# The opening of a Fourier-mixing and hard-swish kernel: x loaded ahead of the weights, dummy products between its pieces, and a first chunk of plain block products

## The chip, the cores and the metric

The kernel runs on one core of one Trainium2 chip, as one launch. The metric is the device time of that launch in microseconds (us). PE is TensorE, ACT is ScalarE, DVE is VectorE, POOL is GpSimd; SP and POOL issue the DMAs. PSUM is the memory, divided into banks, that TensorE's products land in. The granted clock is the share of full speed that TensorE's clock had; at half clock a pass of an fp32 product over 512 columns takes 0.86 us in these traces, at full clock 0.43. "Before" and "changed" are the two kernels compared.

## The reference, cut to what matters

```python
# x: (8, 3008, 256); w_in: (256, 2048); w_out: (2048, 256), all float32
X = np.fft.fft(np.fft.fft(x, axis=1), axis=2).real      # (8, 3008, 256)
h = X.reshape(24064, 256) @ w_in
g = h * np.clip(h + 3.0, 0.0, 6.0) / 6.0
out = g @ w_out
```

The kernel does the length-3008 transform as 47 x 64: a first transform over 47 points, a trip through DRAM, a second over 64 points; the transform over the 256 columns is folded into `w_in`. Two batch rows form a pair, so there are four pairs; each pair has chunks of 256 columns, and each chunk eight steps. The weights arrive with 64 bits an element, as float64 would need; their exponents and mantissas are taken apart and put together as fp32 on ScalarE, TensorE and VectorE, in 16 pieces of 512 KB. Three words recur: the fold of an x piece is VectorE's elementwise work on it ahead of the first transform, the fold of `w_in` is a group of eight TensorE passes, and a join is VectorE's multiplying of a weight piece's mantissa and exponent.

## The kernel before: the parts that matter

Dummy products keep TensorE's clock up where it has no work:

```python
def keep_awake(n):
    ps = ps_h.tile([P, 2 * TB], F32, tag="uv", name="awake")
    for i in range(n):
        nc.tensor.matmul(ps[:], ones[:], Z[:], start=True, stop=True)   # 128x512, fp32
```

The opening takes the eight pieces of x in order. Each brings one piece of weights and moves one through its stages:

```python
for c in range(NXC):                       # NXC = 8
    if c + 2 < NXC:
        load_x(first, c + 2)
    load_w(c + 2)
    if c < NXC - 1:
        fold_first(first, c)               # VectorE
    else:
        for part in range(2):
            fold(first, c, part, nc.vector)    # the odd piece: a longer fold
    on_scalar(c)                           # exponents of a weight piece
    on_vector(c)                           # its mantissa; joins the piece before
    for i in range(XC // 2):
        (stage1_first if c < NXC - 1 else stage1)(first, c, i)    # first transform
    on_tensor(c)                           # exponent product; folds w_in, mixes w_out
    # ... (cut: loads of a table and of a row of w_in)
load_g(first, 0)                           # results read back from DRAM
for j in range(NXC, 15):                   # seven more weight pieces
    # ... (cut: load_w)
    on_scalar(j)
    on_vector(j)
    keep_awake(1)
    on_tensor(j)
# ... (cut)
keep_awake(2)
for i in range(2):
    stage2(first, 0, i)                    # second transform
```

A step is `mlp1` (products u and v, then the activation), `combine` (sums on GpSimd) and `mlp2` (seven products of 256 columns, in the manner of Strassen, in place of eight, on blocks of `w_out` that were mixed beforehand):

```python
for s, (p, ck, fc) in enumerate(steps):
    # ... (cut: what runs beside, for the next pair)
    if s + AHEAD < len(steps):             # AHEAD = 2
        mlp1(*chunk(s + AHEAD))
    if s + 1 < len(steps):
        combine(*chunk(s + 1))
    # ... (cut: store of the last chunk)
    mlp2(*chunk(s))
```

## Time and profile before

| | before |
|---|---|
| time, median of 3 runs | 1981.34 us (1980.88 to 1983.05) |
| span in the profile | 1978.3 us |
| TensorE busy | 1949.1 us, 99% |
| second chunk's first output products start at | 134.96 us |
| TensorE idle from 135 to 1940 us | 4.7 us |

### The profile page before, as it was taken

Reading aid. Unit: us, or ns where it says so; the run is one execution under the profiler, and the core shown is the slowest. Engines: PE = TensorE matmul, PEld = TensorE weight load, DVE = VectorE, ACT = ScalarE, POOL = GpSimd, SP = SyncE. Lnnn points to the kernel's source line nnn. Section 1 sums busy time; section 2 is a strip of 40 time slices with the busy share of each in tenths; the row PEclk is TensorE's granted clock in tenths of the full one; section 3 lists DMA queues with packets and bytes.
Section 4 is the critical chain, followed back from the end, with each engine's and each line's share of the span. In section 5 each row is a group of like instructions: output and inputs, shape, how many; then the busy total and the mean of one; then the engine's idle time right before and its main releaser. Section 6 shows DMA issues by size and latency. Waiting matters only on the chain.

```text
span 1978.3 us, 27746 instructions
## 1 busy us (share of the span) xinstructions
PE 1949.1 (99%) x9178; PEld 1685.4 (85%) x9178; DVE 1433.5 (72%) x2775; ACT 687.9 (35%) x1164; POOL 1414.2 (71%) x1604
## 2 busy tenths in 40 slices
PE   8899999999999999999999999999999999999998
PEld 5588888888998888888898888888889888888887
DVE  5677767776787776776777776777678777777776
ACT  6533333333333333333333333333333333333332
POOL 4277778786687787777768877778667667666765
PEclk9999999999999999999999999999999999999999
DMA  9502211111111111221111221212110101111000
GB/s 307 136 26 61 51 41 46 49 49 35 27 36 51 41 49 48 54 59 24 36 32 30 63 55 44 56 41 54 37 22 23 30 14 25 26 24 28 17 20 20
DMA packets 149701, 93.31 MB, mean 47 GB/s; under 512 B 121739, under 2 KB 135055, under 8 KB 149558
## 3 DMA queue, kind: packets, MB, share of 16 engines
q1 hardware_dynamic: 139294, 57.86, 12.2%
q0 software_dynamic: 9472, 33.49, 5.9%
q8 instruction: 72, 1.18, 0.2%
q14 instruction: 71, 0.58, 0.1%
q10 hardware_dynamic: 792, 0.20, 0.0%
HBM read 54.19 MB, written 37.33 MB: 46 GB/s over the span
## 4 chain that ended last, share of the span: by engine, by line
PE 93%; DVE 2%; ACT 1%; issue 0%; DMA 0%; SPq 0%; DVEq 0%; ACTq 0%
PE acc L403 56%; PE v L334 16%; PE u L334 16%; PE ps L284 2%; PE ps L227 2%; DVE a L379 1%; DVE s L339 1%; ACT t L376 0%; ACT PM L509 0%; DVE o L461 0%; PE wps L574 0%; DVE u L360 0%; PE ps L224 0%; PE ex L514 0%; PE awake L597 0%
## 5 line engine op out<-in xcount | busy, mean ns | idle before, releaser
L393 POOL TENSOR_TENSOR c<-a 128x512 f32<-128x512 f32 (+1 forms) x383 | 478.2, 1248 | 431.4 <-PE acc L403 369.3
L403 PE MATMUL acc<-c,G 128*128 128x256 f32 (+1 forms) x3072 | 712.0, 375 | 0.0
L376 ACT ACTIVATE t<-u,half 128x512 f32<-128x512 f32 (+1 forms) x384 | 261.0, 680 | 1100.5 <-DVE u L349 1018.7
L403 PEld LDWEIGHTS acc<-c,G 128*128 128x128 f32 x3072 | 577.5, 190 | 72.7
L339 DVE SCALAR_TENSOR_TENSOR s<-qn,WN,u 128x256 f32<-128x256 f32 (+1 forms) x768 | 330.0, 471 | 354.3 <-PE u L334 354.0
L403 PE MATMUL acc<-a,G 128*128 128x256 f32 (+1 forms) x2304 | 551.2, 375 | 0.0
L403 PEld LDWEIGHTS acc<-a,G 128*128 128x128 f32 x2304 | 433.8, 190 | 55.9
L334 PE MATMUL v<-q,W 127*128 127x256 f32 (+1 forms) x1536 | 390.1, 376 | 4.4 <-DVE a L379 4.4
L334 PE MATMUL u<-q,W 128*128 128x256 f32 (+1 forms) x1536 | 388.3, 375 | 2.4 <-DVE a L379 2.1
L379 DVE SCALAR_TENSOR_TENSOR a<-t,u 128x512 f32<-128x512 f32 (+2 forms) x448 | 263.7, 600 | 104.9 <-ACT t L376 102.1
L334 PEld LDWEIGHTS u<-q,W 128*128 128x128 f32 x1536 | 285.7, 190 | 58.2 <-issue 14.8
L334 PEld LDWEIGHTS v<-q,W 127*128 127x128 f32 x1536 | 288.7, 190 | 45.1 <-DVE a L379 4.1
L393 POOL TENSOR_TENSOR c<-c,a 128x256 f32<-128x256 f32 (+1 forms) x383 | 274.8, 717 | 30.0
L393 POOL TENSOR_TENSOR c<-a,c 128x256 f32<-128x256 f32 (+1 forms) x383 | 274.6, 717 | 30.1
L349 DVE TENSOR_TENSOR u<-s,v 128x512 f32<-128x512 f32 x352 | 245.0, 696 | 37.7 <-PE v L334 0.8
L379 DVE SCALAR_TENSOR_TENSOR a<-t,v 128x512 f32<-128x512 f32 (+1 forms) x480 | 263.2, 564 | 0.0
L376 ACT ACTIVATE t<-v,half 128x512 f32<-128x512 f32 (+1 forms) x384 | 260.5, 678 | 0.0
L351 DVE TENSOR_TENSOR v<-v,s 128x512 f32<-128x512 f32 x352 | 243.7, 692 | 0.0
L393 POOL TENSOR_TENSOR r<-w,e 128x256 f32<-128x256 f32 (+1 forms) x94 | 90.8, 987 | 3.7
L411 ACT ACTIVATE e<-acc 128x512 f32<-128x512 f32 (+2 forms) x190 | 86.3, 545 | 3.4 <-PE acc L403 3.3
L461 DVE STREAM_TRANSPOSE o<-r 128x256 f32<-128x256 f32 (+1 forms) x192 | 72.5, 414 | 0.2
L239 ACT COPY z<-ps 96x512 f32<-96x512 f32 x64 | 37.2, 582 | 83.7 <-PE ps L227 65.2
(91 smaller groups left out, 780.2 us busy)
## 6 DMA issues: line engine op xcount, KB each, us to landing
out_dram<-o SPq DMA_DIRECT2D x746, 32.0 KB
zd<-z SPq DMA_DIRECT2D x32, 384.0 KB
g<-zd SPq DMA_DIRECT2D x48, 256.0 KB
xt<-in_x_dram POOLq DMA_DIRECT2D x21, 384.0 KB, 4.1
qn<-qd SPq DMA_DIRECT2D x19, 256.0 KB
st<-in_moe_w_in_dram POOLq DMA_DIRECT2D x8, 512.0 KB, 9.1
st<-in_moe_w_out_dram POOLq DMA_DIRECT2D x8, 512.0 KB, 5.1
xt<-in_x_dram POOLq DMA_DIRECT2D x7, 376.0 KB, 3.9
```

Of the source, the lines that this page charges most:

```text
L227: nc.tensor.matmul(ps[0:PZ], F[0:PR, 0:PZ], y[:, 2 * i:2 * i + 2, :], start=True, stop=True)
L284: nc.tensor.matmul(ps[:, blk, u * P:n].rearrange("p (b k) -> p b k", b=2), g[:, kk, blk * (P + 1):blk * (P + 1) + P], T[:, :, gr, blk, kk, ...
L334: nc.tensor.matmul(ps[:, i, 0:nq], W1[r, blk, f * P:(f + 1) * P], q[r, blk, of:of + nq], start=True, stop=True)
L339: nc.vector.scalar_tensor_tensor(s[:, i, 0:nq], qn[:, of:of + nq], WN[:, f:f + 1], u[:, i, 0:nq], op0=AL.mult, op1=AL.add)
L349: nc.vector.tensor_tensor(u[:], s[:], v[:], op=AL.add)
L351: nc.vector.tensor_tensor(v[:], v[:], s[:], op=AL.subtract)
L376: nc.scalar.activation(t, h, AF.Relu, bias=half[:], scale=scale)
L379: nc.vector.scalar_tensor_tensor(dst, t, 1.0, h, op0=AL.min, op1=AL.mult)
L393: (eng or nc.gpsimd).tensor_tensor(out, in0, in1, op=AL.add)
L403: nc.tensor.matmul(ch.acc[i // 2][:, i % 2, 0:ch.n], G[:, i, fc, :], mv, start=(fc == 0 and i % 2 == 0), stop=(fc == NF - 1), skip_group_c ...
L411: nc.scalar.mul(ch.e[:, k:i + 1, 0:ch.n], ch.acc[i // 2][:, 0:i + 1 - k, 0:ch.n], 1.0 / WS)
L461: nc.vector.transpose(o[:, 0:n // DH, h], ch.r[:, m, h, 0:n].rearrange("p (j i) -> p j i", i=DH))
```

## The change

What the code does, with its aims as I read them: x is asked for ahead of the weights, so that the first transform ends early; dummy products between the pieces keep the clock up while TensorE waits; the weights are made ready partly before the second transform and partly around the first chunk's steps; and the first chunk multiplies by the four plain blocks of `w_out`, eight products in place of seven, so that it needs no mixed blocks and no sums. The core of the diff, with cuts marked:

```diff
-    keep_awake(6)
+    keep_awake(13)
 # ... (cut)
+    order = [NXC - 1] + list(range(NXC - 1))
+    for c in order[0:6]:
+        load_x(first, c)
+    load_forward(first, order[6])
+    for k, c in enumerate(order):
         # ... (cut: folds, as before)
         for i in range(XC // 2):
-            (stage1_first if c < NXC - 1 else stage1)(first, c, i)
-        on_tensor(c)
+            (stage1_first if k > 0 else stage1)(first, c, i)
+        keep_awake(2)
+        # ... (cut: the other x loads, weight pieces 0 to 6 behind them)
+    head(0)                              # exponents and mantissa of a piece
+    for j in range(5):
+        exponent_b(j)
+        keep_awake(2)
+        exponent_c(j)
+        fold_all()
+        if j < 4:
+            head(j + 1)
+        join(j)
+        copy_all()
         # ... (cut)
+    DUE = [(7, 8), (9, 10), (11, 12), (13, 14), (15,), (), (), ()]
 # ... (cut: pieces 5 and 6 around mlp1 of step 0, with keep_awake(3))
+        if s < NF:                       # the first chunk, NF = 8
+            for j in DUE[s][:1]:
+                head(j)
+            copy_all()
+            mlp1(*chunk(s + 1))
+            for j in DUE[s][:1]:
+                tail(j)                  # exponent product, join, next load
+            for j in DUE[s][1:]:
+                head(j)
+            mlp2_first(*chunk(s))        # four products of 512 columns
+            for j in DUE[s][1:]:
+                tail(j)
+            fold_all()
+            if s >= 4:
+                mix_w_out(s - 4)         # now on GpSimd
```

The second pair's loads start eight steps later and come at one piece of x in 8 steps in place of 9.

More of the change, by code (lines that the diff above doesn't have):

```diff
@@ L51 @@
 NK1 = (N1 + 1) // 2
+B11, B21, B12, B22 = 0, 1, 3, 6
 PROD = ("P1", "P2", "-P4", "P5", "P7", "-P6", "P3")
@@ L124, in __init__, with x_tile @@
             self.g, self.q, self.qn = {}, {}, {}
-    def x_tile(pr, i):
+    def x_tile(pr, c, i):
+        i += 2 * (c if pr.p > 0 else (c + 1) % NXC)
         pool, tag = xpool, "x"
@@ L140, in load_forward @@
     def load_forward(pr, c):
-        xt = x_tile(pr, 2 * c)
+        xt = x_tile(pr, c, 0)
         nr = PR + 2 if pr.p < NP - 1 else PR
@@ L151, in load_partners @@
     def load_partners(pr, c):
-        xr = x_tile(pr, 2 * c + 1)
+        xr = x_tile(pr, c, 1)
         pr.xr[c] = xr
@@ L231, in evict_z @@
         if i == 0:
-            pool, tag = (gpool, "g") if pr.p == 0 and c % 3 == 2 else (zpool, "z")
+            pool, tag = (gpool, "g") if pr.p == 0 and c % 3 == 1 else (zpool, "z")
             pr.z[c] = pool.tile([PZ, XC, D], F32, tag=tag, name="z")
-            if c == 0:
+            if pr.zd is None:
                 pr.zd = dpool.tile([2, NK1, 2, NS, D], F32, tag="zd", name="zd")
@@ L311, in __init__ @@
             self.last = ck == NCK - 1
+            self.first = ck == 0 and pr.p == 0
             self.final = self.last and pr.p == NP - 1
@@ L393, in add, with mlp2_first @@
         (eng or nc.gpsimd).tensor_tensor(out, in0, in1, op=AL.add)
+    def mlp2_first(ch, fc):
+        a = ch.a.pop(fc)
+        for h in range(2):
+            if fc == 0:
+                ch.acc[h] = ps_a.tile([P, 2, TB], F32, tag="acc", name="acc")
+            for f in range(2):
+                nc.tensor.matmul(ch.acc[h][:], G[:, (B11, B12, B21, B22)[2 * f + h], fc, :], a[:, :, f],
+                                 start=(fc == 0 and f == 0), stop=(fc == NF - 1 and f == 1))
+        if fc == NF - 1:
+            ch.r = epool.tile([P, 2, 2, TB], F32, tag="r", name="r")
+            for h in range(2):
+                for m in range(2):
+                    nc.scalar.mul(ch.r[:, m, h], ch.acc[h][:, m], (1 - 2 * m) / WS)
     def mlp2(ch, fc):
@@ L486, in load_w @@
         kind, n, i = PIECES[j]
-        st = wpool.tile([P, 2 * WB], I32, tag="st", bufs=4, name="st")
+        pool, tag, bufs = (wpool, "st", 4) if j % 7 < 4 else (cpool, "c", None)
+        st = pool.tile([P, 2 * WB], I32, tag=tag, bufs=bufs, name="st")
         o = st[:].bitcast(moe_w_in.dtype)
@@ L511, in exponent_b @@
     def exponent_b(j):
-        ex = ps_h.tile([P, WB], F32, tag="uv", name="ex")
+        ex = ps_h.tile([P, WB], F32, tag="uv", name="ex") if starting[0] else bank([P, WB], "ex")
         for i in range(2):
@@ L537, in join @@
             return
-        b12 = wpool.tile([P, 2, P], F32, tag="b12", bufs=2, name="b12")[:] if i == 0 else None
-        for h, g in enumerate((block(n, 0), b12) if i == 0 else (block(n, 1), block(n, 6))):
+        for h, g in enumerate((B21, B22) if i else (B11, B12)):
             f, e = (t.rearrange("p (c q h e) -> h p c q e", c=2, h=2, e=DH)[h] for t in (frac, ex))
-            nc.vector.tensor_tensor(g.rearrange("p c (q e) -> p c q e", e=DH), f, e, op=AL.mult)
-        if i == 0:
-            w[PIECES[j]] = b12
+            nc.vector.tensor_tensor(block(n, g).rearrange("p c (q e) -> p c q e", e=DH), f, e, op=AL.mult)
     def block(j, i):
         return G[:, i, 2 * j:2 * j + 2, :]
-    def use_pair(j):
-        kind, n, _ = PIECES[2 * j]
-        if kind == "in":
-            fold_w_in(n)
-        else:
-            mix_w_out(n)
     def mix_w_out(j):
-        b12 = w.pop(("out", j, 0))
         g = [block(j, i) for i in range(7)]
-        tt = nc.vector.tensor_tensor
-        tt(g[3], g[0], b12, op=AL.subtract)
-        tt(g[5], g[6], g[3], op=AL.add)
-        tt(g[2], g[5], g[1], op=AL.subtract)
-        tt(g[4], g[6], b12, op=AL.subtract)
+        tt = nc.gpsimd.tensor_tensor
+        tt(g[4], g[B22], g[B12], op=AL.subtract)
+        tt(g[3], g[B11], g[B12], op=AL.subtract)
+        tt(g[5], g[B22], g[3], op=AL.add)
+        tt(g[2], g[5], g[B21], op=AL.subtract)
     def fold_w_in(n):
@@ L571, in fold_w_in @@
         for blk in range(2):
-            ps = bank([P, WB], "wps")
+            ps = bank([P, WB], "wps") if starting[0] else spare[blk]
             for i in range(2):
@@ L579, in copy @@
                 nc.scalar.copy(W1[:, blk, cs], sums[blk][:])
-            nc.sync.dma_start(out=wn[n:n + 1], in_=W1[P - 1:P, 1, cs])
+            nb = WB // P
+            for k in range(nb):
+                f = n * nb + k
+                nc.sync.dma_start(out=WN[:, f:f + 1], in_=W1[P - 1:P, 1, f * P:(f + 1) * P])
         copies.append(copy)
-    def load_wn(n):
-        nb = WB // P
-        nc.sync.dma_start(out=WN[:, n * nb:(n + 1) * nb], in_=wn[n].rearrange("(j p) -> p j", p=P))
     def load_t(gr):
@@ L591, in load_t, with keep_awake @@
             nc.sync.dma_start(out=T[b * N2:(b + 1) * N2, b, gr], in_=c_stage2[:, gr])
-    def keep_awake(n):
-        ps = ps_h.tile([P, 2 * TB], F32, tag="uv", name="awake")
+    def keep_awake(n, ps=None):
+        ps = ps_h.tile([P, 2 * TB], F32, tag="uv", name="awake") if ps is None else ps
         for i in range(n):
@@ L621, with head, tail, fold_all @@
         nc.scalar.copy(t, Z[r].unsqueeze(1).to_broadcast([N2, NG, 2 * TB]))
-    wn = dpool.tile([NWI, WB], F32, tag="wn", bufs=1, name="wn")
-    load_forward(first, 0)
-    load_partners(first, 0)
-    load_w(0)
-    load_x(first, 1)
-    load_w(1)
-    pending, copies = [], []
-    def on_scalar(j):
-        for i in pending:
-            exponent_c(i)
-        if j is not None:
-            exponent_a(j)
+    folds, copies = [], []
+    def head(j):
+        exponent_a(j)
+        mantissa(j)
+    def tail(j):
+        exponent_b(j)
+        exponent_c(j)
+        join(j)
+        if j + 7 < len(PIECES):
+            load_w(j + 7)
+        if j % 2 and PIECES[j][0] == "in":
+            folds.append(PIECES[j][1])
+    def fold_all():
+        while folds:
+            fold_w_in(folds.pop(0))
+    def copy_all():
         while copies:
             copies.pop(0)()
-    def on_vector(j):
-        if j is not None:
-            mantissa(j)
-        for i in pending:
-            join(i)
-    def on_tensor(j):
-        if j is not None:
-            exponent_b(j)
-        done = pending.pop() if pending else 0
-        if done % 2:
-            use_pair(done // 2)
-        if j is not None:
-            pending.append(j)
-    for c in range(NXC):
-        if c + 2 < NXC:
-            load_x(first, c + 2)
-        load_w(c + 2)
-        if c < NXC - 1:
+    order = [NXC - 1] + list(range(NXC - 1))
[3 more added lines that the diff above has]
+    for k, c in enumerate(order):
+        if k > 0:
             fold_first(first, c)
@@ L666 @@
                 fold(first, c, part, nc.vector)
-        on_scalar(c)
-        on_vector(c)
         for i in range(XC // 2):
-            (stage1_first if c < NXC - 1 else stage1)(first, c, i)
-        on_tensor(c)
-        if c == 0:
-            load_t(0)
-        if c in (4, 6):
-            load_wn(PIECES[c - 4][1])
-    load_g(first, 0)
-    for j in range(NXC, 15):
-        if j < 14:
-            load_w(j + 2)
-        on_scalar(j)
-        on_vector(j)
-        keep_awake(1)
-        on_tensor(j)
-    load_wn(PIECES[6][1])
-    load_wn(PIECES[8][1])
-    load_g(first, 1)
-    load_t(1)
-    keep_awake(2)
+            (stage1_first if k > 0 else stage1)(first, c, i)
+        keep_awake(2)
+        if k == 0:
+            load_partners(first, order[6])
+        elif k == 1:
+            load_x(first, order[7])
+            load_t(0)
+            for j in range(4):
+                load_w(j)
+        elif k in (4, 5):
+            for j in ((4, 5), (6,))[k - 4]:
+                load_w(j)
+    load_g(first, 0)
+    head(0)
+    for j in range(5):
+        exponent_b(j)
+        keep_awake(2)
+        exponent_c(j)
+        fold_all()
+        if j < 4:
+            head(j + 1)
+        join(j)
+        copy_all()
+        load_w(j + 7)
+        if j % 2 and PIECES[j][0] == "in":
+            folds.append(PIECES[j][1])
     for i in range(2):
@@ L692 @@
     starting[0] = False
+    spare = [ps_a.tile([P, WB], F32, tag="acc", name="spare") for blk in range(2)]
     chunks = [[Chunk(pr, ck) for ck in range(NCK)] for pr in pairs]
     NST = 2 * NF
-    after = {}
     def beside(p):
@@ L706, in beside @@
         cur = pairs[p]
+        late = 4 if p == 0 else 0
         if p == 0:
-            for f in (on_scalar, on_vector, on_tensor):
-                after.setdefault(1, []).append((f, (None,)))
-            for gr in range(2, NG):
-                after.setdefault(gr, []).append((load_t, (gr,)))
+            put(2, load_g, cur, 1)
+            for gr in range(1, NG):
+                put(gr + 1, load_t, gr)
             put(NF - 1, close_w)
@@ L721, in beside @@
                 put(NST * (gr - 2) + 12, load_g, cur, gr)
-            s2(NST * (gr - 1), cur, gr)
+            s2(NST * (gr - 1) + (late if gr == 1 else 0), cur, gr)
         if p + 1 < NP:
@@ L725, in beside @@
             for c in range(NXC):
-                put(9 * c, load_x, nx, c)
-                put(9 * c + 3, fold, nx, c, 0, nc.gpsimd)
-                put(9 * c + 5, fold, nx, c, 1, nc.gpsimd)
+                t = 2 * late + (9 - late // 4) * c
+                put(t, load_x, nx, c)
+                put(t + 3, fold, nx, c, 0, nc.gpsimd)
+                put(t + 5, fold, nx, c, 1, nc.gpsimd)
                 for i in range(XC // 2):
-                    put(9 * c + 8 + 3 * i, stage1, nx, c, i)
+                    put(t + 8 + 3 * i, stage1, nx, c, i)
             put(NST * (NG - 1) - 2, load_g, nx, 0)
@@ L747, in chunk @@
         return chunks[p][ck], fc
-    on_scalar(15)
-    on_vector(15)
+    DUE = [(7, 8), (9, 10), (11, 12), (13, 14), (15,), (), (), ()]
+    head(5)
     mlp1(*chunk(0))
-    mlp1(*chunk(1))
-    on_tensor(15)
-    combine(*chunk(0))
+    tail(5)
+    head(6)
+    keep_awake(3, spare[0])
+    tail(6)
     prev = None
@@ L760 @@
             f(*a)
-        if s + AHEAD < len(steps):
-            mlp1(*chunk(s + AHEAD))
-        if s + 1 < len(steps):
-            combine(*chunk(s + 1))
-        if prev and fc < 3:
-            finish(prev) if fc == 0 else store(prev, fc - 1)
-        mlp2(*chunk(s))
-        for f, a in after.get(s, ()):
-            f(*a)
+        if s < NF:
[13 more added lines that the diff above has]
+                mix_w_out(s - 4)
+            if s == NF - 1:
+                mlp1(*chunk(NF + 1))
+                combine(*chunk(NF))
+        else:
+            if s + AHEAD < len(steps):
+                mlp1(*chunk(s + AHEAD))
+            if s + 1 < len(steps):
+                combine(*chunk(s + 1))
+            if prev and fc < 3:
+                if fc > 0:
+                    store(prev, fc - 1)
+                elif not prev.first:
+                    finish(prev)
+            mlp2(*chunk(s))
         if fc == NF - 1:
```

## The prediction

> **What bounds the kernel now.** I read the page first, then busy time by stretch, then the chain of work in order of time up to 140 us, then the timeline of the opening on all engines.
>
> ```profile
> PE 1949.1 (99%) x9178; PEld 1685.4 (85%) x9178; DVE 1433.5 (72%) x2775; ACT 687.9 (35%) x1164; POOL 1414.2 (71%) x1604
> ...
> 0.00:10.00 10.00, 8.39 (x12) 3.29 (x12) 2.63 (x9) 7.47 (x5) 6.38 (x13) 1.00 0.81 220
> 10.00:54.00 44.00, 39.73 (x156) 25.41 (x157) 27.51 (x60) 27.28 (x50) 14.15 (x21) 0.94 1.00 314
> 54.00:77.00 23.00, 19.72 (x50) 8.12 (x49) 14.65 (x32) 16.03 (x27) 2.85 (x4) 0.97 0.74 187
> 77.00:92.00 15.00, 10.74 (x53) 8.24 (x52) 9.41 (x18) 6.26 (x10) 5.55 (x7) 0.92 0.33 82
> 92.00:135.00 43.00, 41.54 (x196) 35.92 (x195) 32.22 (x54) 14.13 (x24) 28.10 (x31) 0.99 0.05 15
> 135.00:1940.00 1805.00, 1800.31 (x8549) 1576.79 (x8548) 1320.74 (x2514) 606.60 (x1030) 1339.37 (x1508) 1.00 0.16 39
> ```
>
> The first line is the page's: TensorE is busy 99%. The others are stretches: their length, then busy time of PE, PEld, DVE, ACT and POOL, the granted clock, the DMA share and GB/s. From 135 us on TensorE idles 5 us in 1805, so nothing is to be won there, and the change touches only what lies before. So the question is one date: when does the second chunk's first output product start, and what TensorE work is left then? In the chain of work it is this:
>
> ```profile
> 92.06 3.53 PE acc L403 x14
> 97.31 3.02 PE acc L403 x14
> ...
> 129.34 3.02 PE acc L403 x14
> 132.37 0.86 PE ps L227 x2
> 133.23 0.86 PE u L334 x4
> 134.09 0.86 PE v L334 x4
> 134.96 3.02 PE acc L403 x14
> ```
>
> The first chunk's eight steps start their output products (seven Strassen-like products each) at 92.06 to 129.34, the second chunk's first at 134.96. That step carries the first products (u, v) of two steps ahead and one product of the next pair.
>
> The opening up to there, from the timeline (start, duration, what; in brackets the idle time before):
>
> ```profile
> 1.61 8.39 PE L597 MATMUL awake<-Z,ones 128*128 128x512 f32 x12 [1.61 <-DVE ones L601]
> ...
> 9.11 0.69 DVE L189 TENSOR_TENSOR y<-xt 94x508 f32<-94x508 f32 x1 [5.47 <-DMA xt<-in_x_dram,IX]
> ...
> 13.52 0.68 DVE L189 TENSOR_TENSOR y<-xt 94x508 f32<-94x508 f32 x1 [1.80 <-DMA xt<-in_x_dram,IX]
> ...
> 49.17 1.99 PE L227 MATMUL ps<-y,F 94*96 94x512 f32 x2 [2.87 <-DVE y L174]
> ...
> 71.64 1.40 ACT L509 ACTIVATE PM<-st,bias 128x512 uint8<-128x512 int16 x2
> 73.09 0.38 PE L514 MATMUL ex<-PM,E 128*128 128x512 f16 x1 [0.27 <-ACT PM L509]
> 73.50 0.58 ACT L518 ACTIVATE ex<-ex 128x512 int32<-128x512 f32 x1 [0.46 <-PE ex L514]
> 74.00 1.40 ACT L509 ACTIVATE PM<-st,bias 128x512 uint8<-128x512 int16 x2
> ```
>
> Six dummy products run to 10.0; x's first piece lands at 9.1, the second at 13.5 with a weight piece between. The first transform ends at 53.7 after an idle gap and half-speed products. A weight piece then cycles through ScalarE (1.40), TensorE, ScalarE in 74.00 - 71.64 = 2.36 us.
>
> **What the Trainium skill says.** "TensorE: Matmul & The Clock Gate", Part 1: the array's clock falls to half after an idle window of about 3.4 us and returns after a busy one. The trace agrees in kind: the gap of 2.87 us is followed by 1.99 us for what later takes 0.86 (132.37), and the first dummy passes come 0.86 apart, the later ones 0.43. Same page, Back-to-back issue gap: N/2.4 + 2.5 ns, 216 ns at 512 columns. The fp16 products of the trace keep it (0.21); an fp32 product is two records of 0.43 at 512 columns, so 0.86 us warm. I use the trace's. "SBUF — State Buffer", Who interferes with whom: a VectorE instruction with two SBUF inputs contends with GpSimd's reads. Here the four weight mixing operations take 0.42 each at 70 us, GpSimd idle, and 0.83 to 1.48 at 101 us, GpSimd busy. "DMA: Bandwidth & Descriptors", Issuing engines are not separate DMA queues: all share 16 engines; here they are saturated at 314 GB/s from 10 to 54 us.
>
> **The change part by part**, as one clock through TensorE's new order (which I read from the two built programs, the order of instructions with their waits):
>
> *Start.* 13 dummy products instead of 6: 14 more passes of 0.43 = +6.0, so they end at 16.0. The first x piece (now the last one, folded by the longer form, nine VectorE operations that took 2.95 us before) should land at 9 as now and be folded by 12: the dummies, not the data, set 16.0.
>
> *First transform.* The odd piece takes 2.15 warm (0.86 + 0.43 + 0.86), each of seven others eight passes of 0.43 = 3.43. After every piece two dummies of 0.86 = 1.71. x alone is 0.79 MB a piece, 2.5 us at 314 GB/s, and even with 0.39 MB of results written a piece, 3.8 us: x arrives faster than TensorE goes through a piece, 5.14 us. So the dummies sit on the path. 16.0 + 2.15 + 1.71 + 7 x 5.14 = 55.9; the last real product ends at 54.2 (before: 53.7). What the early x won is spent.
>
> *Five weight pieces before the second transform* (before: fifteen). ScalarE is free at 55.3 after the last eviction. Pieces 0 and 1: exponents 55.3 to 56.7, product to 57.2, next exponents to 59.1, product to 59.5, dummies to 61.0. Piece 2: product to 61.85, dummies to 63.4, fold of w_in (8 passes) to 66.8. Piece 3's product goes behind it, to 67.25; piece 4's exponents wait on ScalarE for the fold's copies (67.6), come at 68.1 to 69.5; product 69.95, dummies 71.45, second fold to 74.9. The results read back for the second transform (sent at 57.4 before, the same now) are long there. Second transform: 16 + 8 passes of 0.107 = 2.6 us, from 74.9 (before 77.4) to 77.5.
>
> *First chunk.* u, v of step 0 to 79.2, activations through 82.1; pieces 5 and 6 interleaved with three dummies (2.6); step 0's output products start at about 86, 6 us before today's 92.06. But each step now has four block products of 512 columns, 8 x 0.43 = 3.43, instead of 3.02 (+0.4 a step, +3.3 in all), one or two exponent products (0.43 each) and in two steps a fold (3.43), which all were done before today's step 0. TensorE's sum a step: 9.4, 9.4, 6.0, 6.0, 5.6, 5.2, 5.2, 5.2. Waits: one PSUM bank serves all exponent products, so piece 8's product waits for piece 7's join (idle about 1.6), piece 9 and 14 the like; I find about 5 us of idle in steps 0 to 4. Starts of output products: 86, 97, 107, 113, 121, 126, 131, 137. Then u, v of steps 8 (in step 7), 9 and 10, and the second chunk's first output product starts at 144.1, against 134.96: **+9.1**. Left over then: one half of the second transform and one first-transform product, 0.86 each, which now come 4 and 8 steps later: **+1.7**. Sum **+10.8**.
>
> *Off the path:* mixing on GpSimd (16 operations of about 0.72) takes VectorE's 1.7 to 4.2 us a block away, but TensorE waits for neither. The first chunk needs no combine.
>
> **Cross-check by TensorE work.** Before 144.1: real work 26.2 first transform, 6.9 exponents, 13.7 folds, 3.4 second transform, 19.0 for u and v, 27.4 outputs = 96.6; dummies 13 + 16 + 10 + 3 = 42 products: 14.4 with the slow start, then 29 x 0.857 = 24.9; in all 137.5 with the 1.6 of start-up. So even with no wait at all 137.5 - 135.0 + 1.7 = +4.2 us. Dummies grow from 17.9 (30 records now) to 39.3: +21.4. That exceeds what can be removed: idle 1.6 + 4.3 + 3.3 + 4.3 + 1.5 = 15.0 in the stretches above, and the slow clock's few us.
>
> **Rivals.** (1) The change wins: dummies only fill waits for x, and with an unbroken clock and an earlier step 0 the chunk comes earlier. For it: step 0 is earlier, and the half clock (0.92 to 0.97 in three stretches) goes. It would need x to take over 5 us a piece, but now pieces come each 4.5 us with 0.52 MB of weights between. If it held, -5 us: 1976. (2) The step waits are worse: the one bank and ScalarE's queue (per early step 2 x 1.96 of exponent work + 1.35 + 1.1 of copies = 6.4 us) bind, gaps of 3 us cool the clock again: +20, 2001. For it: each such gap cooled it before. Against: folds and dummies fill most. (3) GpSimd, mixing late (the last block waits for the last plain product), delays the second chunk's combine: +1 to 2.
>
> **Range and chances.** 1981.3 + 10.8 = 1992.1, so 1992. Floor +4.2 gives 1985.5; waits twice as long as I find give +16 and rival 2 up to 2001. Range 1986 to 2000. Two per cent is 40 us, half of all the opening up to step 0, so within 2% at 0.97; faster 0.01, slower 0.02.
>
> **What would show it.** Right: the second dummy group of the start ends at 16.0 with x folded by 12; first-transform pieces 5.1 us apart with no TensorE idle; second transform near 75; step 0's output near 86; second chunk's first near 144; span after it unchanged but for 1.7. Wrong: TensorE idle waiting for x in the first 50 us (dummies free), granted clock below 0.95 after 80 us, or a later stretch that lost or gained over 2 us.

## The result, and the profile after

| | before | changed |
|---|---|---|
| time, median of 4 runs | 1982.19 us (1980.88 to 1984.15) | 1998.17 us (1996.26 to 1998.33) |
| ratio | | 1.0078, 95% interval 1.0060 to 1.0095 |
| span in the profile | 1978.3 us | 1996.3 us |
| second chunk's first output products | 134.96 us | 149.40 us |

Ratios here are the mean time of one kernel's fast runs over that of the other's fast runs of the same rounds, so not quite the ratio of the medians quoted. The changed kernel is 16 us slower by the medians; inside 2%, and clear of noise.

Busy time by stretch of the changed kernel: start and end, length, then busy time of PE, PEld (weight loads), DVE, ACT and POOL with their counts, granted clock, DMA share, GB/s.

```profile
0.00:10.00 10.00, 8.39 (x14) 3.62 (x15) 2.19 (x8) 7.42 (x5) 6.57 (x13) 1.00 0.80 196
10.00:54.00 44.00, 44.00 (x167) 27.65 (x166) 14.22 (x34) 10.82 (x22) 10.90 (x16) 1.00 0.89 264
54.00:77.00 23.00, 22.48 (x75) 10.96 (x74) 7.89 (x14) 13.82 (x23) 3.04 (x5) 1.00 0.56 156
77.00:92.00 15.00, 13.30 (x44) 6.93 (x43) 12.19 (x23) 10.93 (x18) 2.29 (x4) 1.00 0.37 105
92.00:135.00 43.00, 39.72 (x119) 21.18 (x118) 33.06 (x61) 21.64 (x35) 11.18 (x14) 0.96 0.21 56
```

From 10 to 54 us TensorE is busy without a gap at full clock, where it idled 4.3 us before, and yet the first transform ends no earlier. DMA went the other way, from a share of 1.00 to 0.89: with TensorE full, the transfers have slack. The chain of work of the changed kernel, in order of time (start, length, what):

```profile
1.60 14.11 PE awake L609 x26
15.72 0.86 PE ps L231 x2
...
50.56 3.46 PE ps L204 x16
...
74.59 1.78 PE ps L288 x16
...
96.75 3.43 PE acc L408 x8
...
109.28 4.54 PE acc L408 x6
...
149.40 3.02 PE acc L424 x14
```

"awake" are dummies, "ps L204" is the first transform, "ps L288" the second, "acc L408" a step's plain products, "acc L424" the second chunk's first. The two dates of the last two rows are what the prediction did not have. Between them and the first lines, how TensorE and VectorE go through one piece of x:

```profile
22.88 1.88 PE L609 MATMUL awake<-Z,ones 128*128 128x512 f32 x4
23.08 0.68 DVE L193 TENSOR_TENSOR y<-xt 94x508 f32<-94x508 f32 x1 [3.79 <-PE ps L204]
23.69 0.68 DVE L194 TENSOR_TENSOR xt<-xt 94x508 f32<-94x508 f32 x1
24.29 0.17 DVE L195 TENSOR_TENSOR xt<-xt 94x8 f32<-94x8 f32 x1
24.60 0.60 PE L204 MATMUL ps<-xt,F 94*96 94x258 f32 x2
```

In brackets is the idle time before an instruction and what ended it. Before the change, the fold waited for "DMA xt"; now VectorE idles 3.79 us at each piece and what ends it is TensorE's own products. x is there; TensorE's queue is what x waits for, and the dummies are in that queue.

The span grew by 18.0 us. Of this, 14.4 us are in the date of the second chunk. The next 1.7 us are one second-transform half and one first-transform product (0.86 each) that now come after that date. Some 1.5 us more is a wait: over the next 370 us, TensorE waits for ScalarE to empty the one PSUM bank that both transforms share. First the kernel before, then the changed one (who waits for whom: us in total, times, longest):

```profile
PE ps L227 <- ACT q L287: 1.2, 2, 0.7
```

```profile
PE ps L231 <- ACT q L291: 2.7, 4, 0.7
```

These three make 17.6 of 18.0.

### The profile page after: what moved, and what is told of

The parts are those of the page before. It is cut to its first block, busy times and chain, and to the rows that moved or that the text cites. A ratio compares the mean times of both kernels' runs of the same rounds, so it can differ in the third digit from the quotient of the medians.

```text
span 1996.3 us, 27723 instructions
## 1 busy us (share of the span) xinstructions
PE 1971.9 (99%) x9184; PEld 1684.6 (84%) x9184; DVE 1427.8 (72%) x2759; ACT 687.8 (34%) x1164; POOL 1398.3 (70%) x1591
## 4 chain that ended last, share of the span: by engine, by line
PE 95%; DVE 2%; ACT 1%; issue 0%; DMA 0%; SPq 0%; DVEq 0%; ACTq 0%
PE acc L424 54%; PE v L339 16%; PE u L339 16%; PE ps L288 2%; PE ps L231 2%; PE awake L609 1%; PE ps L204 1%; PE acc L408 1%; DVE a L384 1%; DVE s L344 1%; ACT PM L532 0%; ACT t L381 0%; DMA out_dram<-o 0%; DVE o L482 0%; PE wps L587 0%
## 5 line engine op out<-in xcount | busy, mean ns | idle before, releaser
L398 POOL TENSOR_TENSOR c<-a 128x512 f32<-128x512 f32 (+1 forms) x375 | 467.5, 1247 | 401.0 <-PE acc L424 366.6
L424 PE MATMUL acc<-c,G 128*128 128x256 f32 (+1 forms) x3008 | 697.0, 375 | 0.0
L424 PEld LDWEIGHTS acc<-c,G 128*128 128x128 f32 x3008 | 565.4, 190 | 71.1
L424 PE MATMUL acc<-a,G 128*128 128x256 f32 (+1 forms) x2256 | 539.0, 375 | 0.0
L424 PEld LDWEIGHTS acc<-a,G 128*128 128x128 f32 x2256 | 424.1, 190 | 54.4
L398 POOL TENSOR_TENSOR c<-c,a 128x256 f32<-128x256 f32 (+1 forms) x375 | 268.4, 716 | 29.4
L398 POOL TENSOR_TENSOR c<-a,c 128x256 f32<-128x256 f32 (+1 forms) x375 | 268.2, 715 | 29.4
```

The lines of the kernel that those rows point to most:

```text
L398: (eng or nc.gpsimd).tensor_tensor(out, in0, in1, op=AL.add)
L424: nc.tensor.matmul(ch.acc[i // 2][:, i % 2, 0:ch.n], G[:, i, fc, :], mv, start=(fc == 0 and i % 2 == 0), stop=(fc == NF - 1), skip_group_c ...
```

## The experiments

Times are medians of four to six runs; the record holds no e9 or e10. The kernel before was run beside them each time: its median was 1980.3 to 1980.6 us in these rounds, so 1 to 2 us below that in the table above, and a ratio is safer than a difference of medians across rounds. By the ratio alone e2, e4 and e7 (1.0072 to 1.0075, each about 0.0014 either way) can't be told from the changed kernel (1.0060 to 1.0095); what is said of them rests on one trace each. The last column is the date at which the second chunk's output products start in the profiled run. Such a date has a scatter of its own: the 13 dummies of the start, the same in the changed kernel, e1, e4 and e7, took 14.11, 13.55, 13.18 and 13.54 us, so up to 0.9 us of a difference can be theirs.

| run | what it is | time, us | ratio to before | second chunk at |
|---|---|---|---|---|
| (changed) | | 1998.17 | 1.0078 | 149.40 |
| e1 | changed, no dummies between x pieces | 1988.79 | 1.0041 | 140.06 |
| e2 | changed, 9 dummies at the start | 1995.51 | 1.0074 | 146.35 |
| e4 | changed, no dummies in the weight loop | 1995.37 | 1.0072 | 146.69 |
| e6 | changed, all three | 1983.99 | 1.0023 | 135.26 |
| e3 | before, with dummies between x pieces | 1988.85 | 1.0039 | 143.81 |
| e5 | before, with the plain first chunk | 1979.88 | 1.0001 | 138.55 |
| e8 | before, odd x piece first | 1980.76 | 0.9997 | 138.01 |
| e7 | changed, other order of weight pieces | 1995.59 | 1.0075 | 147.23 |
| e13 | e6, that order, old pace of the next pair | 1986.45 | 1.0024 | 139.44 |
| e11 | before, fewer dummies | 1978.84 | 0.9988 | 136.74 |
| e12 | e11 with plain chunk and dummies in waits | 1978.62 | 0.9983 | 133.98 |
| e14 | e12 with x one piece further ahead | 1977.82 | 0.9980 | 132.85 |

The theory at the start was that of the prediction: the dummies lie on TensorE's path. The rivals were that they only fill waits, and that other parts of the change make the loss.

### e1: no dummies between the pieces of x

```diff
             (stage1_first if k > 0 else stage1)(first, c, i)
-        keep_awake(2)
```

> The changed kernel without the two dummy products after each of the eight x pieces. Theory (dummies are on TensorE's path, x arrives faster than it is used): 8 x 1.71 = 13.7 us go, less some waits for x since a piece of x with its results (1.18 MB) needs 3.8 us of DMA against 3.43 of TensorE: 10 to 13.7 us less than the changed kernel, 1984 to 1988, the second transform starting at 61 to 65. Rival (dummies filled waits for x or kept the clock up): 0 to 3 us less, 1995 to 1998, with TensorE idle before each piece or a granted clock well below 1 from 16 to 55 us.

It took 9.4 us off, by the medians, and 9.3 off the date. So the dummies are on the path, and the rival (0 to 3 us) falls; but I had expected 10 to 13.7. What bounds it now, in its chain of work:

```profile
21.41 10.04 DMA zd<-z
...
32.62 12.11 DMA zd<-z
```

These are the writes of the first transform's results to DRAM. With the dummies gone TensorE is ahead, the DMA share in that stretch is 0.99, each write takes over 10 us to land, and its buffer, one of few, is wanted again. I had counted the bytes a piece, but put them at a wait for x; the wait that came was for the results' buffers. The granted clock fell to 0.92 there, and that cost 1.1 us on the chain: the first two dummies of the weight loop took 2.85 us in place of 1.72. The second transform started at 66.96, later than the 61 to 65 that I had expected and 7.6 us earlier than in the changed kernel. The other 1.7 us of the date are gained at step 2. Its wait of 2.04 us is as in the changed kernel (shown at e7), but the six passes after it ran at full clock:

```profile
101.64 2.84 PE L408 MATMUL acc<-a,G 128*128 128x512 f32 x6 [2.04 <-DVE G L564]
```

The changed kernel took 4.54 us for them. So 7.6 us, not 9.3, were gained up to the second transform, where these dummies stood, and 0.56 of that is a start that ended earlier; why the clock held at step 2 stays open.

### e2: nine dummies at the start

```diff
-    keep_awake(13)
+    keep_awake(9)
```

> The changed kernel with 9 dummy products at the start instead of 13. Theory (the start's dummies, not the data, set when the first transform begins: the fold is ready at 12): 4 x 0.86 = 3.4 us less, about 1994.7, first real product at 12.3. Rival (the data come later than the dummies end, or the clock cools): no change, 1998.

The first real product starts at 12.13 us in place of 15.72, and the date moves by 3.05 us. By time it is 2.7 us under the changed kernel by the medians; the ratio moves by 0.0004 only, because the kernel before ran faster in these rounds. The date, inside one execution, speaks for the theory. TensorE now waits 0.89 us for the fold of x ahead of that product, so the data are the next bound.

### e3: the dummies between the pieces put into the kernel before

```diff
             (stage1_first if c < NXC - 1 else stage1)(first, c, i)
+        keep_awake(2)
```

> The kernel before, plus two dummy products after each of its eight x pieces: that part of the change alone. Theory: 13.7 us of TensorE work, of which it can hide at most the 4.3 us that TensorE idles there between 10 and 54 us: 9 us slower, less up to 2 for the half clock at 49 us that goes: 1989 to 1991. Rival (they only fill waits): 1981 to 1984.

8.5 us slower than before, ratio 1.0039 (1.0026 to 1.0053), and the date is 8.85 later. TensorE's idle time from 10 to 54 us fell from 4.3 to 0.9, and the last piece's products, at half clock before, took 2.2 us in place of 4.6: of 13.7 us of dummies, about 3.4 went into idle time, 2.3 came back by the clock, and most of the rest went onto the path. The second transform starts at 84.53 in place of 77.54, 7.0 us later; the other 1.9 us of the date come after it, at a granted clock of 0.88 from 92 to 135 us. So the same part of the change costs about the same on both kernels at the second transform: 7.0 us here, 7.1 in e1 (7.6 less the 0.56 at its start).

### e4: no dummies in the weight loop

```diff
         exponent_b(j)
-        keep_awake(2)
         exponent_c(j)
 # ...
-    keep_awake(3, spare[0])
```

> The changed kernel without the dummies in the loop over the first five weight pieces and without the three ahead of step 0. Theory: pieces 0, 1, 3 are bound by ScalarE's cycle of 2.36 us, so only the two groups ahead of the folds are on the path: 2 x 1.71 = 3.4 us less, 1994 to 1995.5. Rivals: all five groups and the three are on the path: 8.6 + 2.6 = 11 less, 1987; or the clock cools in the gaps and it is as slow as now or slower.

2.8 us less by the medians and 2.71 by the date, where 3.4 was expected; 0.94 of the 2.71 is not the edit's, since the start's dummies happened to end that much earlier (14.78 against 15.72). The rival of 11 us falls: all groups on the path would have meant a ratio near 1.002, and the interval is 1.0059 to 1.0086. That only the groups ahead of the folds were on the path fits, but the gain is too small to settle it by time. Something was given back, and TensorE's timeline shows it:

```profile
57.07 0.38 PE L537 MATMUL ex<-PM,E 128*128 128x512 f16 x1 [1.33 <-ACT PM L532]
57.73 0.38 PE L537 MATMUL ex<-PM,E 128*128 128x512 f16 x1 [0.28 <-ACT PM L532]
59.43 0.38 PE L537 MATMUL ex<-PM,E 128*128 128x512 f16 x1 [1.33 <-ACT PM L532]
60.08 0.59 PE L537 MATMUL ex<-PM,E 128*128 128x512 f16 x1 [0.27 <-ACT PM L532]
60.46 4.95 PE L587 MATMUL wps<-wi,C 128*128 128x512 f32 x8
```

No gap here is longer than 1.33 us, but TensorE works less than half of the time, and the fold that follows takes 4.95 us in place of 3.60, which fits first passes at half clock. So the other dummies of the loop do earn something, 1.35 us here.

### e6: the three together

e1, e2 and e4 in one kernel.

> The changed kernel with 9 dummies at the start and none between the x pieces, in the weight loop or before step 0. Theory (the dummies' cost, and nothing else of the opening, but without them the DMA engines set the first transform, as the run without the piece dummies showed): its gain of 9.4 and the loop's 2.8 add, the start's 2.7 only as far as DMA lets it: 12 to 15 us less than the changed kernel, 1983 to 1986, so still slower than before: what is left (2 to 5 us) is the first chunk, which prepares eleven weight pieces on the way. Rival (dummies are the whole loss, or more): 1977 to 1981.

1984.0, inside the expected 1983 to 1986. The date is 135.26, 14.1 us earlier than in the changed kernel, and only 0.3 later than before. The three single gains (9.3, 3.05, 2.7) add to 15.1. So of the 14.4 us that the opening lost, 14.1 go with the dummies; 1.7 of these are step 2's half clock, which is gone here as in e1 (six passes in 2.84 us after the same wait). All else in the change together (the order of the loads, the plain products, the weights around the steps) comes out even up to that date, within the scatter of dates; that its parts are even one by one isn't shown. What remains of the loss, 3.9 us in the span, is mainly the work deferred beyond it, with its bank waits.

### e5: the plain first chunk in the kernel before

The four-block products of the first chunk, no sums for it, and the mixing of `w_out` on GpSimd from step 4 on; the rest as before.

```diff
-        mlp2(*chunk(s))
+        (mlp2_first if s < NF else mlp2)(*chunk(s))
+        if 4 <= s < NF:
+            mix_w_out(s - 4)
```

> The kernel before with the plain block products in its first chunk and the mixing on GpSimd: that part of the change alone. Theory: 3.3 us more TensorE work; against it the mixing leaves VectorE (1.65 us ahead of the last fold of x, and the pieces of 0.8 to 1.5 us at 101 to 105 us that stall a step by 1.5) and step 0 needs no combine: within 2 us of before, 1979 to 1983. Rival (plain products are a loss as large as their work): 1984 or more. Rival (they are the gain the change is for): below 1978.

Ratio 1.0001 (0.9987 to 1.0015): even, though the interval leaves room for 2 to 3 us either way. Of the 3.3 us of longer products (3.44 against 3.02 a step, eight times) its trace shows 1.5 paid back: the 1.46 us that TensorE waits for "DVE a" ahead of the fourth step's products in the kernel before, behind VectorE's mixing, is gone. That the rest is paid is not shown. The one profiled execution was 3.3 us longer than the median, so its date is not a good measure here.

### e7: the second pair of w_out pieces earlier

In the changed kernel step 2's products wait for blocks of `w_out` made from pieces 10 and 11, which are joined just ahead of it. TensorE's timeline of the changed kernel:

```profile
106.22 1.02 PE L408 MATMUL acc<-a,G 128*128 128x512 f32 x2
109.28 4.54 PE L408 MATMUL acc<-a,G 128*128 128x512 f32 x6 [2.04 <-DVE G L564]
```

Two passes, then 2.04 us of waiting for "DVE G", the join, and then six passes in 4.54 us, where e1 takes 2.84 after the same wait.

```diff
-    PIECES = [("in", 0), ("in", NWI // 2), ("out", 0), ("in", 1), ("in", NWI // 2 + 1)]
-    PIECES = [... for k, n in PIECES + [("out", j) for j in range(1, NWO)] ...]
+    PIECES = [("in", 0), ("in", NWI // 2), ("out", 0), ("out", 1), ("in", 1), ("in", NWI // 2 + 1)]
+    PIECES = [... for k, n in PIECES + [("out", j) for j in range(2, NWO)] ...]
```

> The changed kernel with the second pair of w_out pieces made ready before the second and fourth pair of w_in (order of pieces only). In the changed kernel step 2's output products wait 2.04 us for these blocks and then run at half clock (4.54 us for six passes instead of 2.57). Theory (the extra over my sum is this wait): 4 us go, 1 comes back where u, v of step 4 wait for the copies of the last w_in fold: 2 to 4 us less, 1994 to 1996. Rival (the wait only moves): 1998.

2.6 us less by the medians, 2.2 by the date, of which 0.57 is a start that happened to end earlier: part went, part came back as a new wait. Its chain shows a 1.98 us DMA of a row of the folded `w_in`, which step 4 now waits for.

### e8: the odd piece first in the kernel before

```diff
-    for c in range(NXC):
+    for k, c in enumerate(order):        # order: 7, 0, 1, ... 6
```

> The kernel before with the odd x piece taken first instead of last: that part of the change alone. Theory: its long fold (2.95 us) then lies in the start-up and no longer in TensorE's gap of 2.87 us before the last piece, whose products ran at half clock (4.96 instead of 2.15): 3 to 6 us less than before, 1975 to 1978. Rival (DMA, saturated to 54 us, sets the end of the first transform in any case): 1979 to 1982.

No gain: ratio 0.9997 (0.9984 to 1.0010). The rival had the time right, but the trace does not show DMA holding the end of the first transform. What was won at the end was lost at the start: x's first piece took 7.72 us to land instead of 5 or 6, its long fold followed, and TensorE's first real product came at 14.27, after 4.23 us of idle time, where it came at 10.53 before. The products after that gap ran at half clock (1.79 us for what takes 0.86). From there to the last piece TensorE ran without a break, then waited 0.87 us (products at 51.47) for a fold that VectorE began at 50.01, straight behind its mixing of weights (from 48.42 on) and not after a wait for x. So the late start, and TensorE's own work from there, set the end in this run, although the DMA share was 1.03.

### e13: few dummies, the other order, and the old pace for the next pair

The edit of e7 in e6, and the next pair's loads and folds from step 0 on, one piece in 9 steps.

```diff
-                t = 2 * late + (9 - late // 4) * c
+                t = 9 * c
```

> The changed kernel with few dummies (1984.0), the second w_out pair earlier, and the next pair's loads and transforms at the old pace of one x piece in 9 steps from step 0. Theory: 1.5 to 2.6 us less from the order of pieces, 1.5 less because first and second transform no longer wait for the same PSUM bank: 1980 to 1981.5. Rival (the pace costs nothing): 1982 to 1983; the order without the clock's fall gives nothing: 1984.

A miss: 1986.5, where e6 has 1984.0; by the ratios (1.0024 and 1.0023) no better and no worse than e6. Its bank waits fell from 2.7 to 1.9 us, but the first chunk lost more. Its timeline:

```profile
80.50 2.93 DVE L549 TENSOR_SCALAR top<-st 128x512 int32<-128x512 int32 x1
80.81 1.27 POOL L170 TENSOR_TENSOR xt<-xt 94x508 f32<-94x508 f32 x1
82.03 1.09 POOL L171 TENSOR_TENSOR xt<-xt 94x508 f32<-94x508 f32 x1
```

A mantissa operation of VectorE that takes 0.42 us elsewhere took 2.93, until GpSimd was through two operations on the next pair's x (83.12); TensorE then waited 3.84 us for "DVE wi". "SBUF — State Buffer", Who interferes with whom, in the Trainium skill, says that a `tensor_scalar` in a two-port mode and a GpSimd instruction block each other fully, whoever issued first having the ports; the 2.93 us agrees in kind. That the operation ran in such a mode isn't shown, and the trace dates its start 0.31 us ahead of GpSimd's. This is a likely reason for the change's eight steps of delay, argued from this trace: the next pair's folds then keep clear of the weights.

### e11: fewer dummies in the kernel before

```diff
         on_vector(j)
-        keep_awake(1)
+        if j not in (9, 11):
+            keep_awake(1)
         on_tensor(j)
 # ...
     load_t(1)
-    keep_awake(2)
```

> The kernel before, without the dummies that its chain of work shows on the path: those right behind the two w_in folds (0.86 each) and the two ahead of the second transform (1.72). Those that fill ScalarE's cycle stay. Theory (a dummy costs its length where TensorE would not wait, nothing where it would): 3.4 us less than before, 1976 to 1978, unless the granted clock falls. Rival (TensorE waits for ScalarE there anyway): 1980.

1978.84, with a ratio of 0.9988 (0.9972 to 1.0004): likely a gain, not clear of noise. The kernel before varies more from run to run (1979.45 to 1984.39 in these rounds) than the changed one (1996.26 to 1998.33). In e11's profiled run the last x piece's products started at 52.26, against 49.17 in the one of before, though nothing differs up to there. That saturated DMA makes the scatter is not shown: e3, with the dummies between the pieces, still spread over 4.2 us, and e1, which waits for DMA writes, over 1.7.

### e12: dummies where TensorE waits

e11 and e5 together, and two dummies in each of the two waits of about 2 us that TensorE has ahead of step 0:

```diff
+    spare = ps_a.tile([P, 2 * TB], F32, tag="acc", name="spare")
     mlp1(*chunk(0))
+    keep_awake(2, spare)
     mlp1(*chunk(1))
     on_tensor(15)
+    keep_awake(2, spare)
```

> As the run before it in this call, with the plain products of the first chunk and the mixing on GpSimd too, and two dummies in each of TensorE's two waits of about 2 us ahead of step 0, after which u, v and the first products ran at half clock. Theory: 3.4 us from the first part, nothing from the plain products, 1.5 to 2.5 us from the clock: 1974 to 1977, faster than both kernels. Rival (the dummies delay u and v): 1977 or more.

1978.62, ratio 0.9983 (0.9970 to 0.9996): faster than both kernels, though by less than I expected. Busy time by stretch, of e5 and then of e12, in the two stretches that these dummies are for:

```profile
77.00:92.00 15.00, 10.47 (x53) 7.45 (x52) 9.86 (x16) 6.68 (x11) 1.74 (x2) 0.99 0.39 99
92.00:135.00 43.00, 43.00 (x140) 25.82 (x139) 27.84 (x50) 12.21 (x21) 13.90 (x18) 0.96 0.02 6
```

```profile
77.00:92.00 15.00, 13.93 (x61) 9.25 (x60) 10.97 (x20) 7.32 (x12) 1.45 (x2) 1.00 0.34 92
92.00:135.00 43.00, 43.00 (x148) 26.55 (x147) 27.58 (x50) 12.79 (x24) 18.00 (x23) 1.00 0.02 7
```

The granted clock is 1.00 from 77 us on, and step 0's products take 3.44 us, where e5's take 4.18. From the start of the second transform to the date e12 takes 57.5 us, and so does e14, which has these dummies too; e5 takes 59.2. The same kind of dummy that lies on the path between x's pieces pays here, by 1.6 us as far as these traces show.

### e14: x one piece further ahead

e12, with each x piece asked for one piece earlier.

```diff
     load_x(first, 1)
+    load_x(first, 2)
     load_w(1)
 # ...
-        if c + 2 < NXC:
-            load_x(first, c + 2)
+        if c + 3 < NXC:
+            load_x(first, c + 3)
```

> As the run with the plain products and the dummies in the waits (1978.6), with each x piece asked for one piece earlier, so ahead of one more piece of weights: the first part of the change in a mild form. There the last x piece lands at 49.5 us and holds TensorE, DMA being saturated; x, its results, eight weight pieces and the tables are some 14.5 MB, 47 us at the measured 306 GB/s. Theory (x ahead is the part of the change that is worth something where TensorE waits for it): the last piece's products start 2 to 4 us earlier and the time falls by 1 to 4 us, 1974.5 to 1977.5. Rival (weights that come later hold the loop after it by as much): 1978 to 1979.

1977.82, ratio 0.9980 (0.9965 to 0.9994): faster than before, but not to be told apart from e12 (1978.62). The last piece's fold began at 49.97, against 49.54 in e12: x came earlier, but the weight pieces came later, and VectorE, whose program has a weight piece ahead of that fold, waited for it (0.99 us for "DMA st"). So the products did not start earlier, as the theory had it (52.59, against 52.16). They ended 1.1 us earlier all the same, at full clock after a wait of 1.15 us, where e12's ran at half clock after one of 2.74; the date is 1.13 earlier. Of all kernels run it has the lowest median.

## Why the prediction was right, point by point

The measured 1998.17 is within the range of 1986 to 2000; the predicted 1992 was 6 us low. The predicted change was +10.8, the measured one +16.0 by the medians and +18.0 between the two profiled runs.

| step of the prediction | predicted | profile |
|---|---|---|
| start's dummies end, first real product | 16.0 | 15.72 |
| first transform's last product ends | 54.2 | 54.0 |
| second transform starts | 74.9 | 74.59 |
| output products of steps 0, 1 | 86, 97 | 85.76, 96.75 |
| of step 2 | 107 | 106.2, then held to 109.28 |
| of step 3 | 113 | 116.47 |
| of steps 4 to 7 | 121, 126, 131, 137 | 124.32, 129.48, 134.65, 140.71 |
| second chunk's first | 144.1 | 149.40 |
| work left over | +1.7 | 1.7 |
| rest of the span | 0 | +1.5 bank waits, and 0.4 |

*Dummies on the path.* Right in kind, and the dates to step 1 hold within 0.4 us. e1 and e3 show it on both kernels, e2 for the start. The full price of the piece dummies, 13.7 us, is not what one gets back on taking them out, though: e1 got 7.6 up to the second transform, because the results' writes become the bound, and 1.7 at step 2 by the clock.

*Rival 1,* an unbroken clock and a full TensorE win: the clock did stay at 1.00 up to 92 us, and TensorE did stay full up to 54, and the time went up. A full TensorE was not the aim; it was filled with dummies.

*The step whose size was off:* "I find about 5 us of idle in steps 0 to 4". It held them in the wrong places: the dates predicted from step 0 to step 5 (86 to 126, for 36.4 us of work) leave room for 3.6 us, and the three longest waits measured there are 0.94, 2.04 and 1.05, 4.0 in all. Two waits were not in it. Step 2's products need the join of pieces 10 and 11, which the predicted 107 does not wait for: 2.04 us. Step 10's v waits at the change to the second chunk for a PSUM bank, held by an activation still to come: 1.53 us, ended by "DVE a". And after the first of them the products ran at half clock, for 1.7 us more (4.54 against the 2.84 that e1 and e6 took after the same wait). These sum to 5.3, and the date is 5.3 later than predicted. Rival 2, that the step waits are worse and cool the clock, was right in kind and in part; e7 took about 1.6 of these us away by the order of pieces alone (2.2 by the date, less 0.57 at the start).

*Rival 3,* GpSimd's late mixing: it does finish late, at 145.8 us, and the second chunk's first sums start at 145.73 right behind it; they are ready for its products at 149.40. No cost shown.

*Left out:* the wait for the bank shared by both transforms, 1.5 us, since I took the span after 135 us as unchanged. That the new pace of the next pair is its cause is only argued: e13, with the old pace, has 1.9 us of it, between the two.

*What stays open:* the 0.4 us of rest; why the clock fell after step 2's wait of 2.04 us in the changed kernel, e2 and e4, and not in e1 and e6; and how much of e12's gain is due to each of its three parts, since e11 alone was not clear of noise.

## What to carry to other kernels

In these runs a dummy product cost up to its whole length where TensorE would not have waited, and earned something only where it would have: so look, before putting one in, at what ends the wait of the work that follows it, and at who is waiting for whom once it is in. An opening is best judged by one date further on, and by what is left after that date, not by how early a single stage starts: here step 0 came 6 us earlier, because eleven of the sixteen weight pieces came after the second transform in place of one, and the second chunk came 14 us later. And the gain from taking work away ends at the next bound, here DMA at a share of 0.99, so single costs read off a chain were upper limits of what came back.

## What the Trainium skill lacked or had wrong

- "TensorE: Matmul & The Clock Gate", Part 1 and the advice on gaps: it names idle windows of about 3.4 us and tells to avoid idle gaps of over about 3 us. Here single gaps of 2.87 us (before) and 2.04 us (changed) were followed by half-speed products, while the same gap of 2.04 us in e1 and e6 was not; and in e4 gaps of no more than 1.33 us, with TensorE at work less than half of the time between them, led to a fold of 4.95 us in place of 3.60. So the length of one gap did not settle it in these runs. The page does speak of short idle times that come often, but has no figure for how long or how many.
- The same page, Back-to-back issue gap: its formula fits the fp16 products (0.21 us at 512 columns), but it has no word on fp32, which takes four times that here (0.86 us for a product, two records of 0.43). "FP8 and Floating Point Precision" does say that true fp32 makes four passes; the runs agree.
- "DMA: Bandwidth & Descriptors", Latency and other measured facts, gives about 2 us of fixed cost. With the DMA share at 0.99, a 384 KB write took 10.0 and 12.1 us to land (e1): in an opening the queue ahead of a transfer counts for more than the fixed cost. The page's tables have no figure for transfers that queue.
